# Attention, ELU layer and Sinkhorn mixture on one core: order of the sums' copies, a VectorE transpose for the gate, and four small moves

## The chip, the cores and the metric

The kernel runs on one core of one Trainium2 chip. A core has five engines that each work through their own list of instructions in order: PE (TensorE, matrix products), DVE (VectorE), ACT (ScalarE), POOL (GpSimd) and SP (SyncE, here only a queue that issues DMAs). They wait for one another by semaphores. The metric is the device time of one execution in microseconds (us); less is better.

## The reference

```python
# attention: B=4, H=8, S=576, D=64, causal window of 64
scores = where(0 <= i - j < 64, q @ k.T / 8, -1e9)
x = softmax(scores) @ v                      # -> 2304 tokens x 512
# layer 1: 512 -> 2048 -> 512 with ELU
h = x @ w_in;  x = elu(h) @ w_out
# layer 2: 8 experts, 512 -> 1024 -> 512
P = exp(x @ w_gate - max)
for _ in range(8):                           # Sinkhorn
    P /= P.sum(1, keepdims=True) + 1e-9
    P /= P.sum(0, keepdims=True) + 1e-9
    P *= N / E
out = sum over e of P[:, e] * (relu(x @ w1[e]) @ w2[e])
```

The weights `w_in` and `w_out` come as float64 and are turned into float32 on the chip. Each float32 operand is split into a high and a low part, and each product is done as three products (high x high, high x low, low x high).

## The kernel before

The 2304 tokens are five blocks, four of 512 and the last of 256. Program order per engine is written out by hand, so what stands in an engine's list is what the code emits, in that order.

Attention (to about 180 us) works on 48 groups, two in each step `m`. In a step the code emits transposes of q and k (`pair_T`, tiles `ptr`, `qkT`), scores (`grp_S`, tile `s`), exponentials (`grp_E`), and products with v (`grp_V`, tile `pv`). V is needed a second time shifted by 64 rows: `v_load` brings `vo`, `v_shift` makes `ve` from it, by GpSimd for the first two pairs of heads and by two DMAs on SP's queue after that. For every third pair `vo` is a part of the tile `acc`. `warm(n)` emits products of zeros. Chunks of layer 1 fill the slots between.

Layer 1's first quarter ends with the last block: `m0_in` and `m0_out` (tiles `p`). `elu` makes the activated block `gh` and its low part `gl`, spread over three later moments (`run_later`). Between the last block's first and second products one chunk of the next quarter, `step_in(steps[0])`, is emitted.

The gate follows layer 1 block by block: `gate_a` makes the logits transposed (`lg`, 16 rows of which 8 are of the weights' high and 8 of their low part), `gate_b` turns them by products with a small selection matrix `sel` into `Lg`, tokens by experts. `sink_parts` is then a list of small steps, maximum (`mx`, `nb`), exponential, and alternately `rows` and `cols`, that are emitted one at a time between chunks of layer 2. `cols` sums over tokens by a product (`csum`) and makes the factor `rc`.

The last stage (from about 866 us) does the experts by a Strassen-like scheme. For each of 38 periods there are 14 first-layer chunks `l1` (six products of 384 columns into `la` or `lb`) and 7 second-layer products `l2` (18 products of 256 columns into `oa` or `ob`), two chunks and one product a step `s`, the products `LAG` steps behind. After a chunk ScalarE keeps a copy of its accumulator (`keep`: `a`, `u`, `v`; and `r`), and only then may the next chunk into the same accumulator run. VectorE makes sums from these (`c`, `s`), and of each sum ScalarE makes the high part `h` (`hid`), VectorE or GpSimd the low part (`hid_low`); those are what the second-layer products read. The list `after` holds work that is emitted behind the next chunk; in the kernel before it holds the last sum of each half period alone.

SP's list is in program order too, and a DMA that waits there holds up all behind it.

Of the kernel before, what the change touches and what calls it, by code (L numbers as in the profile page):

```python
# [8 lines left out]
F32 = mybir.dt.float32  # L9
# [9 lines left out]
def kernel(  # L19
# [42 lines left out]


    mask = const.tile([P, P], F32, name="mask")
    sel = const.tile([2 * E, E], F32, name="sel")
    gwr = const.tile([P, NCC, E], F32, name="gwr")
    pad_cm, pad = pool("pad", side="right")
    ctx.callback(close, pad_cm)
# [42 lines left out]
    def ps_sm(name):  # L111
        return ps.tile([P, 512], F32, tag="sm", bufs=1, name=name)
# [144 lines left out]
    def pair_load(pi):  # L257
        b, hp = divmod(pi, NPAIR)
        h0 = 2 * hp
        t = {}  # L260
        for z, (nm, src) in enumerate((("q", q), ("k", k))):
            if pi % 3 == 2:
                w = NTQ * 2 * D
                x = acc[3][:TQ, z * w:(z + 1) * w].rearrange("p (t h d) -> p t h d", h=2, d=D)
            else:
                x = at.tile([TQ, NTQ, 2, D], F32, tag="nat", bufs=4, name=f"{nm}n")
            for h in range(2):
                nc.sync.dma_start(
                    out=x[:, :, h, :],
                    in_=src[b, h0 + h].rearrange("(t p) d -> p t d", p=TQ),  # L270
                )
            t[nm] = x
        qk_nat[pi] = t
# [267 lines left out]
    def moe1_out(st, extra):  # L541
        step_out(st)
        u, j, i = st
        if u == NU - 1 and i == UF - 1:
            fs = [
                lambda: (x2_store(j), x2_split(j, (0, 1))), lambda: x2_split(j, (2, 3)),
                lambda: None, lambda: gate_a(j), lambda: gate_b(j),
            ]
            logits.append(fs[3])
            gate_fs.extend(fs)  # L550
            extra += fs
            if j == len(blocks) - 2:
                extra += sink_parts()


    lgT = {}
# [1 line left out]
    def gate_a(j):  # L558
        n = blocks[j][1]
        lg = ps_sm("lg")  # L560
        for c in range(NCC):
            nc.tensor.matmul(lg[:, :n], gw[:, c, :], Xh[j][:, c, :], start=(c == 0), stop=False)
            nc.tensor.matmul(
                lg[:, :n], gw[:, c, :], Xl[j][:, c, :], start=False, stop=(c == NCC - 1)
            )
        t = work.tile([P, TB], F32, tag="m", bufs=2, name="lgT")[:2 * E]
        nc.vector.tensor_copy(t[:, :n], lg[:2 * E, :n])
        lgT[j] = t

    def gate_b(j):  # L570
        t0, n = blocks[j]
        lt = ps_sm("lt")
        nt = n // P
        t = lgT.pop(j)
        for tt in range(nt):
            nc.tensor.matmul(
                lt[:, tt * E:(tt + 1) * E], t[:, tt * P:(tt + 1) * P], sel, start=True, stop=True
            )
        nc.vector.tensor_copy(
            Lg[:, t0 // P:t0 // P + nt, :], lt[:, :nt * E].rearrange("p (t e) -> p t e", e=E)  # L580
        )

    sk = {}

    def sink_parts():
# [35 lines left out]
        def cols():  # L621
            t = ps_sm("csum")
            nc.tensor.matmul(t[:, :E], ones, sk["cs"], start=True, stop=True)
            rc = sk["rc"]
            nc.vector.tensor_scalar(rc, t[:, :E], 1e-9, None, op0=ALU.add)
            nc.vector.reciprocal(rc, rc)
            nc.vector.tensor_scalar(rc, rc, float(NT) / E, None, op0=ALU.mult)
            nc.vector.tensor_tensor(
                out=Pr, in0=Pr, in1=rc.unsqueeze(1).to_broadcast([P, NTT, E]), op=ALU.mult
            )  # L630
# [402 lines left out]
    def l1(k, n, p, pi):  # L1033
# [27 lines left out]
        def ssum(nm, a, b, op):  # L1061
            d[nm] = tmp("s", 6, nm)
            nc.vector.scalar_tensor_tensor(d[nm], d[a], 0.0, d[b], op0=ALU.max, op1=op)  # L1063

        if pi == 1:
            keep("a")
        elif pi == 2:
            add("c11", "a")
            hid_low(*hid(key, 0, d["c11"], True))
        elif pi == 6:  # L1070
            keep("u")
        elif pi == 5:
            keep("v")
            c = d["C"][:, :TH]
            t = tmp("c", 5, "c22")
            nc.vector.tensor_tensor(out=t, in0=c, in1=d["v"], op=ALU.add)  # L1076
            d["c22"] = t
            hid_low(*hid(key, 2, t, True))
        elif pi == 3:
            d["r21"] = tmp("s", 6, "r21")  # L1080
            nc.scalar.activation(d["r21"], o, AF.Relu)
            ssum("s3", "c11", "r21", ALU.subtract)
            h3 = hid(key, 5, d["s3"], False)
            ssum("s1", "c22", "r21", ALU.add)
            ssum("s2", "c11", "s1", ALU.subtract)
            h2 = hid(key, 4, d["s2"], False)
            h1 = hid(key, 3, d["s1"], False)
            for h in (h3, h2, h1):
                hid_low(*h)
        elif pi == 4:  # L1090
            add("c21", "u")
            h1 = hid(key, 1, d["c21"], True)
            ssum("s4", "c21", "s2", ALU.add)
            hid_low(*h1)
            after.append(lambda: hid_low(*hid(key, 6, d["s4"], False)))
            del chains[key]


# [50 lines left out]
    with tc.manual_schedule():  # L1149
# [25 lines left out]
        warm(8)  # L1175
        for n in range(2):
            pair_T(n)
            warm(2)
        for kk in range(2 * UF):
            bg += w_tasks(kk)  # L1180
        NGRP = B * NPAIR * NG
# [31 lines left out]
        for m in range(NST + 3):  # L1213
# [23 lines left out]
                grp_N(mid)  # L1237
            for n in nxt:
                pair_T(n)
            for n in old:  # L1240
                if n > NG and n % NG == 0:
                    v_shift(n // NG)
            if fin:
                pv = ps_ac("pv")
# [10 lines left out]
                bg += [w_tasks(2 * UF + x)[0] for x in range(2)]  # L1255
            run_bg(rate[1])
            run_later()
            for n in new:
                if n and n % NG == 0:
                    v_load(n // NG)  # L1260
            for pi in range(3, B * NPAIR):
                if 3 * pi // 2 - 4 == m:
# [8 lines left out]
        nc.gpsimd.tensor_tensor(  # L1271
            out=gw[:, :, E:2 * E], in0=gwr, in1=r(gw[:, :, 0:E]), op=ALU.subtract
        )
        nc.vector.tensor_copy(sel[0:E, :], ident[0:E, 0:E])
        nc.sync.dma_start(out=sel[E:2 * E, :], in_=ident[0:E, 0:E])
        run_bg(len(bg))
        bg += [w_tasks(2 * UF + m)[1] for m in range(2)]
        for kk in range(2 * UF + 2, 4 * UF):
# [5 lines left out]
        while avail:  # L1284
            for _ in range(min(2, len(avail))):
                if avail[0][:2] == ("o", len(blocks) - 1) and not queue:
                    step_in(steps[0])
                    queue.append(steps[0])
                    run_later()
                run_sub(avail.pop(0))  # L1290
            run_bg(2)
            run_later()
            run_bg(2)
            run_later()
# [6 lines left out]
        for s, st in enumerate(steps):  # L1301
            u, j, i = st
            su = s % per_u
            if su == 0 and u + 1 < NU:
                for kk in range(2 * UF):
                    bg += w_tasks(2 * UF * (u + 1) + kk)
            if s:
                step_in(st)
                queue.append(st)
            rate = 0 if su < 3 else 5  # L1310
# [108 lines left out]
        for s in range(NPD * 7 + LAG):  # L1419
            k, j = divmod(s, 7)  # L1420
            if k < NPD:
                for z, (p, pi) in enumerate(pairs[j]):
                    l1(k, s * 2 + z, p, pi)
                    if pi != 4:
                        while after:
                            after.pop(0)()
                    w1_load(s * 2 + z + NW1)
            while after and k >= NPD:
                after.pop(0)()
            if s == LAG - 1:  # L1430
                l2(0, 0)
            elif s > LAG:
                l2(*divmod(s - LAG, 7))
# [50 lines left out]
```

## Time and profile before

| | before |
|---|---|
| three runs, us | 2008.22, 2011.4 (median), 2015.02 |
| profiled execution, us | 2014.06 |
| its span, us | 2011.6 |
| PE busy in it | 1989.5 us, 99% |
| DVE, ACT, POOL busy | 69%, 43%, 38% |
| DMA, mean over the span | 239 GB/s |

The span is from the first to the last instruction of the profiled execution; its own time is 2.5 us longer. A share of busy time is a mean over stages that differ: attention fills ACT, the normalisation fills DVE, and most of the rest fills PE.

### The profile page before, as it was taken

What the parts mean: (1) busy time and instruction counts of PE and PEld (TensorE: products, weight loads), DVE (VectorE), ACT (ScalarE), POOL (GpSimd) and SP (SyncE); (2) the same over time, 40 slices, a digit from 0 to 9 for tenths busy, and PEclk for the clock granted to TensorE, in tenths of its full rate; (3) what the DMA queues carried; (4) which work ended last, traced back from release to release, by engine and by line L of the source; (5) the groups of instructions that cost most, each with busy time, mean ns of one, the idle gap of its engine ahead of it and who ended that gap; (6) DMA issues with size and microseconds to landing.
All of it is one profiled execution on the core that took longest, in us unless ns stands there. A gap on an engine that the chain in (4) does not pass through costs nothing.

```text
span 2011.6 us, 36449 instructions
## 1 busy us (share of the span) xinstructions
PE 1989.5 (99%) x13190; PEld 1844.9 (92%) x13190; DVE 1394.1 (69%) x2727; ACT 860.6 (43%) x1839; POOL 755.7 (38%) x725
## 2 busy tenths in 40 slices
PE   9999999999999999999999999999999999999998
PEld 7778888898888888889999999999999999999998
DVE  6745676767698665657776776767777767777676
ACT  8766455555443443333343333333333333333332
POOL 5323232334255555343363332332344323333332
PEclk9999999999999999999999999999999999999999
DMA  9751254458599999958878878778788788887784
GB/s 212 160 106 40 76 177 155 164 187 294 203 364 337 369 364 367 333 196 270 277 247 270 250 250 247 252 250 248 247 276 274 247 245 250 250 250 248 249 247 128
DMA packets 290866, 481.59 MB, mean 239 GB/s; under 512 B 78528, under 2 KB 145152, under 8 KB 286848
## 3 DMA queue, kind: packets, MB, share of 16 engines
q1 hardware_dynamic: 290608, 479.24, 74.7%
q8 instruction: 105, 1.72, 0.3%
q14 instruction: 73, 0.60, 0.1%
q10 hardware_dynamic: 80, 0.03, 0.0%
HBM read 348.14 MB, written 126.88 MB: 236 GB/s over the span
## 4 chain that ended last, share of the span: by engine, by line
PE 83%; DVE 5%; issue 4%; DMA 3%; ACT 3%; POOL 1%; SPq 1%; DVEq 0%; POOLq 0%; ACTq 0%
PE la L1046 15%; PE oa L1119 13%; PE ob L1119 13%; PE lb L1046 11%; PE ac L884 2%; PE ac L883 2%; PE ac L885 2%; PE p L867 2%; PE p L866 2%; PE p L865 2%; PE p L205 2%; PE p L206 2%; PE p L204 2%; PE ac L532 2%; PE ac L533 2%
## 5 line engine op out<-in xcount | busy, mean ns | idle before, releaser
L1028 POOL TENSOR_TENSOR h<-s,h 128x384 fp32r<-128x384 f32 x304 | 373.4, 1246 | 714.4 <-ACT h L1019 506.6
L1046 PE MATMUL la<-xf,w1f 128*128 128x384 f32 x1824 | 363.1, 337 | 6.8 <-ACT u L1059 6.2
L1046 PEld LDWEIGHTS la<-xf,w1f 128*128 128x128 f32 x1824 | 312.6, 189 | 9.8 <-ACT u L1059 8.6
L1119 PE MATMUL oa<-w2f,h 128*128 128x256 f32 x2394 | 307.3, 282 | 0.8 <-DVE acc L1140 0.8
L1119 PE MATMUL ob<-w2f,h 128*128 128x256 f32 x2394 | 307.2, 282 | 0.0
L1119 PEld LDWEIGHTS oa<-w2f,h 128*128 128x128 f32 x2394 | 302.0, 190 | 1.0 <-DVE acc L1140 1.0
L1119 PEld LDWEIGHTS ob<-w2f,h 128*128 128x128 f32 x2394 | 302.0, 190 | 0.0
L1024 DVE SCALAR_TENSOR_TENSOR h<-c,h 128x384 fp32r<-128x384 f32 x228 | 194.2, 852 | 129.9 <-ACT h L1019 120.9
L1046 PE MATMUL lb<-xf,w1f 128*128 128x384 f32 x1368 | 275.1, 335 | 0.2 <-DVE c L1076 0.2
L1046 PEld LDWEIGHTS lb<-xf,w1f 128*128 128x128 f32 x1368 | 237.7, 189 | 0.7 <-DVE c L1076 0.7
L1019 ACT ACTIVATE h<-s 128x384 fp32r<-128x384 f32 x304 | 150.7, 519 | 181.2 <-DVE s L1063 101.4
L1140 DVE SCALAR_TENSOR_TENSOR acc<-oa,Pr,acc 128x256 f32<-128x256 f32 x393 | 165.2, 475 | 43.1 <-PE oa L1119 43.1
L1019 ACT ACTIVATE h<-c 128x384 fp32r<-128x384 f32 x228 | 117.8, 517 | 171.7 <-DVE c L1054 113.4
L1140 DVE SCALAR_TENSOR_TENSOR acc<-ob,Pr,acc 128x256 f32<-128x256 f32 x381 | 160.2, 475 | 38.3 <-PE ob L1119 38.3
L704 POOL TENSOR_TENSOR sw<-rw 128x256 f32<-128x256 f32 x110 | 103.8, 943 | 208.5 <-DVE f L734 158.1
L246 ACT ACTIVATE hh<-p 128x512 fp32r<-128x512 f32 (+1 forms) x80 | 39.3, 491 | 196.7 <-PE p L867 196.7
L1059 ACT ACTIVATE v<-la 128x384 f32<-128x384 f32 x76 | 37.4, 492 | 198.2 <-PE la L1046 198.2
L1063 DVE SCALAR_TENSOR_TENSOR s<-c,s 128x384 f32<-128x384 f32 x152 | 98.1, 646 | 16.1 <-DVE s L1063 0.5
L865 PE MATMUL p<-xh,f 128*128 128x512 f32 (+1 forms) x320 | 108.6, 339 | 0.0
L867 PE MATMUL p<-xh,f 128*128 128x512 f32 (+1 forms) x320 | 107.6, 336 | 0.0
L866 PE MATMUL p<-xl,f 128*128 128x512 f32 (+1 forms) x320 | 107.5, 336 | 0.0
L247 DVE SCALAR_TENSOR_TENSOR hl<-p,hh 128x512 fp32r<-128x512 f32 (+1 forms) x80 | 44.3, 556 | 89.7 <-ACT hh L246 89.7
(159 smaller groups left out, 3639.6 us busy)
## 6 DMA issues: line engine op xcount, KB each, us to landing
w1f<-wdi SPq DMA_DIRECT2D x532, 256.0 KB, 3.8
w2f<-wdo SPq DMA_DIRECT2D x266, 512.0 KB, 4.1
wdo<-f SPq DMA_DIRECT2D x28, 1024.0 KB, 7.4
rw<-in_moe_w_dram SPq DMA_DIRECT2D x220, 128.0 KB, 4.4
wdi<-f SPq DMA_DIRECT2D x27, 1024.0 KB, 6.8
wdo<-f SPq DMA_DIRECT2D x28, 768.0 KB, 5.3
wdi<-f SPq DMA_DIRECT2D x27, 768.0 KB, 5.0
raw<-in_moe_w_in_dram SPq DMA_DIRECT2D x16, 512.0 KB, 4.4
```

Source lines behind the costliest of these rows:

```text
L247: nc.vector.scalar_tensor_tensor(gl[:, :n], p1[:, :n], 0.0, r(gh[:, :n]), op0=ALU.max, op1=ALU.subtract)
L704: nc.gpsimd.tensor_tensor(out=sw[:, o], in0=a, in1=b, op=op)
L865: nc.tensor.matmul(p1[:, :n], w[:, s, 0, cs], xh, start=(c == 0), stop=False)
L866: nc.tensor.matmul(p1[:, :n], w[:, s, 0, cs], xl, start=False, stop=False)
L867: nc.tensor.matmul(p1[:, :n], w[:, s, 1, cs], xh, start=False, stop=(c == NCC - 1))
L1019: nc.scalar.activation(h[:, 0], src, AF.Relu if relu else AF.Copy)
L1024: nc.vector.scalar_tensor_tensor(h[:, 1], src, 0.0, r(h[:, 0]), op0=ALU.max, op1=ALU.subtract)
L1028: nc.gpsimd.tensor_tensor(out=h[:, 1], in0=src, in1=r(h[:, 0]), op=ALU.subtract)
L1046: nc.tensor.matmul(o, w[:, a, c, :], x[:, b, c, :], start=first and c == 0 and z == 0, stop=last and c == 1 and z == 2, skip_group_check=True,
L1063: nc.vector.scalar_tensor_tensor(d[nm], d[a], 0.0, d[b], op0=ALU.max, op1=op)
L1119: nc.tensor.matmul(o[:, c * HB2:(c + 1) * HB2], hs[p][:, a, c * P:(c + 1) * P], w[:, p, b, :], start=fresh and c != 1 and p == 0 and z == ...
L1140: nc.vector.scalar_tensor_tensor(a, src, pe, a, op0=ALU.mult, op1=ALU.add)
```

## The change

Six edits:

1. Start: the first pair's k is loaded from ScalarE's DMA queue; the two `warm(2)` behind the first two transposes are gone.
2. Third V (pair 2): loaded and shifted one step `m` sooner.
3. Last block of layer 1: two chunks, `steps[:2]`, instead of one stand between its two kinds of products; the main loop then starts at the third.
4. Gate: VectorE transposes 32 rows of the logits in blocks of 32x32, adds the two parts into the attention's `mask` tile, and four DMAs on SP's queue put them into `Lg`. `sel` and the `lt` products are gone.
5. Sinkhorn: one more empty step ahead of it; `cols` does its factor in one VectorE instruction fewer.
6. Last stage: all sums' copies go through `after` (`put`), behind the next chunk's own `keep`, but for the chunk `pi == 4`, which lets them wait for one chunk more; the first second-layer product is done at step `LAG - 3` instead of `LAG - 1`.

```diff
-    sel = const.tile([2 * E, E], F32, name="sel")
+    const.tile([P, E], F32, name="gap")
...
-                nc.sync.dma_start(
+                (nc.scalar if pi == 0 and z else nc.sync).dma_start(
...
-                extra += sink_parts()
+                extra += [lambda: None] + sink_parts()
...
-        t = work.tile([P, TB], F32, tag="m", bufs=2, name="lgT")[:2 * E]
-        nc.vector.tensor_copy(t[:, :n], lg[:2 * E, :n])
-        lgT[j] = t
+        t = work.tile([P, TB], F32, tag="m", bufs=2, name="lgT")[:32]
+        nc.vector.transpose(t[:, :n], lg[:32, :n])
+        v = t[:, :n].rearrange("p (t q e) -> p t q e", q=4, e=32)
+        u = mask[:32, :n // 4].rearrange("p (q t e) -> p q t e", q=4, e=E)
+        nc.vector.tensor_tensor(
+            out=u.rearrange("p q t e -> p t q e"), in0=v[:, :, :, 0:E], in1=v[:, :, :, E:2 * E],
+            op=ALU.add,
+        )
+        lgT[j] = u
...
-        for tt in range(nt):
-            nc.tensor.matmul(
-                lt[:, tt * E:(tt + 1) * E], t[:, tt * P:(tt + 1) * P], sel, start=True, stop=True
+        u = lgT.pop(j)
+        for q in range(4):
+            nc.sync.dma_start(
+                out=Lg[32 * q:32 * q + 32, t0 // P:(t0 + n) // P, :], in_=u[:, q]
             )
-        nc.vector.tensor_copy(
-            Lg[:, t0 // P:t0 // P + nt, :], lt[:, :nt * E].rearrange("p (t e) -> p t e", e=E)
-        )
...
-            nc.vector.tensor_scalar(rc, t[:, :E], 1e-9, None, op0=ALU.add)
+            nc.vector.tensor_scalar(
+                rc, t[:, :E], 1e-9, float(E) / NT, op0=ALU.add, op1=ALU.mult
+            )
             nc.vector.reciprocal(rc, rc)
-            nc.vector.tensor_scalar(rc, rc, float(NT) / E, None, op0=ALU.mult)
...
+        def put(slot, nm, relu):
+            after.append(lambda: hid_low(*hid(key, slot, d[nm], relu)))
+
...
-            hid_low(*hid(key, 0, d["c11"], True))
+            put(0, "c11", True)
...
-            hid_low(*hid(key, 2, t, True))
+            put(2, "c22", True)
...
             ssum("s3", "c11", "r21", ALU.subtract)
-            h3 = hid(key, 5, d["s3"], False)
             ssum("s1", "c22", "r21", ALU.add)
             ssum("s2", "c11", "s1", ALU.subtract)
-            h2 = hid(key, 4, d["s2"], False)
-            h1 = hid(key, 3, d["s1"], False)
-            for h in (h3, h2, h1):
-                hid_low(*h)
+            put(5, "s3", False)
+            put(4, "s2", False)
+            put(3, "s1", False)
...
-            warm(2)
...
-            for n in old:
-                if n > NG and n % NG == 0:
+            for n in mid if m == 4 else old:
+                if n > NG and n % NG == 0 and (n // NG > 2 or m == 4):
                     v_shift(n // NG)
...
-            for n in new:
-                if n and n % NG == 0:
+            for n in nxt if m == 2 else new:
+                if n and n % NG == 0 and (n // NG != 2 or m == 2):
                     v_load(n // NG)
...
-                    step_in(steps[0])
-                    queue.append(steps[0])
-                    run_later()
+                    for st in steps[:2]:
+                        step_in(st)
+                        queue.append(st)
+                        run_later()
+                        run_later()
...
-            if s:
+            if s > 1:
                 step_in(st)
...
                 for z, (p, pi) in enumerate(pairs[j]):
+                    fs = list(after) if pi != 4 else []
+                    del after[:len(fs)]
                     l1(k, s * 2 + z, p, pi)
-                    if pi != 4:
-                        while after:
-                            after.pop(0)()
+                    for f in fs:
+                        f()
...
-            if s == LAG - 1:
+            if s == LAG - 3:
                 l2(0, 0)
```

What this does to the engines' lists shows in three places. First, ScalarE at the start of the last stage, from the copy `r` of the first half period to the copy `v` of the second (`h<-c` and `h<-s` are high parts of sums). Before:

```order
L1081 ACTIVATE r_9239<-la 128x384
L1019 ACTIVATE h_9243<-s_9241 128x384
L1019 ACTIVATE h_9249<-s_9247 128x384
L1019 ACTIVATE h_9251<-s_9245 128x384
L1019 ACTIVATE h_9266<-c_9264 128x384
L1019 ACTIVATE h_9284<-c_9282 128x384
L1019 ACTIVATE h_9287<-s_9268 128x384
L1059 ACTIVATE u<-la 128x384
L1059 ACTIVATE v<-la 128x384
```

And of the change:

```order
L1086 ACTIVATE r_9220<-la 128x384
L1021 ACTIVATE h_9253<-s_9222 128x384
L1021 ACTIVATE h_9256<-s_9226 128x384
L1021 ACTIVATE h_9259<-s_9224 128x384
L1021 ACTIVATE h_9262<-c_9236 128x384
L1021 ACTIVATE h_9265<-s_9238 128x384
L1061 ACTIVATE u<-la 128x384
L1021 ACTIVATE h_9278<-c_9251 128x384
L1061 ACTIVATE v<-la 128x384
```

The copy of the second half's first sum, the second `h<-c`, has moved from ahead of `u` to behind it; five copies of the first half's sums still stand ahead of `u`.

Second, PE at the same place, from the chunk behind which `u` is copied to the first second-layer product (its first two rows; `la` and `lb` are chunks). Before:

```order
L1046 MATMUL la<-xf_9071,w1f 128x384 x6
L1046 MATMUL la<-xf_9074,w1f 128x384 x6
L1046 MATMUL lb<-xf_9077,w1f 128x384 x6
L1046 MATMUL la<-xf_8995,w1f 128x384 x6
L1046 MATMUL lb<-xf_9028,w1f 128x384 x6
L1119 MATMUL ob<-w2f,h_9179 128x256 x3
L1119 MATMUL ob<-w2f,h_9284 128x256 x3
```

And of the change:

```order
L1048 MATMUL lb<-xf_9016,w1f 128x384 x6
L1048 MATMUL la<-xf_9052,w1f 128x384 x6
L1121 MATMUL ob<-w2f,h_9170 128x256 x3
L1121 MATMUL ob<-w2f,h_9278 128x256 x3
L1121 MATMUL ob<-w2f,h_9170 128x256 x3
```

The second-layer product has moved ahead of four chunks, of which the first two end the first period and the next two begin the second.

Third, VectorE at the fourth full block's logits, which are the last, and the first step of the Sinkhorn part behind them (`hl`: low part of a layer 2 chunk; `f`: low parts of expert weights). Before:

```order
L567 COPY lgT<-lg 16x512
L247 SCALAR_TENSOR_TENSOR hl<-p_6130,hh 128x512
L579 COPY Lg<-lt 128x32
L591 TENSOR_REDUCE mx<-Lg 128x1
L734 TENSOR_TENSOR f_6167<-rw,f_6167 128x4x256
```

And of the change:

```order
L567 STREAM_TRANSPOSE lgT<-lg 32x512
L570 TENSOR_TENSOR mask<-lgT 32x4x4x8
L247 SCALAR_TENSOR_TENSOR hl<-p_6121,hh 128x512
L736 TENSOR_TENSOR f_6154<-rw,f_6154 128x4x256
L736 TENSOR_TENSOR f_6154<-sw,f_6154 128x4x256
L736 TENSOR_TENSOR f_6171<-rw,f_6171 128x4x256
L736 TENSOR_TENSOR f_6171<-sw,f_6171 128x4x256
L736 TENSOR_TENSOR f_6188<-rw,f_6188 128x4x256
L247 SCALAR_TENSOR_TENSOR hl<-p_6201,hh 128x256
L736 TENSOR_TENSOR f_6188<-sw,f_6188 128x4x256
L247 SCALAR_TENSOR_TENSOR hl<-p_6238,hh 128x256
L901 TENSOR_TENSOR acc_103<-ac,acc_103 128x512 x4
L592 TENSOR_REDUCE mx<-Lg 128x1
```

The reduction `mx`, the first reader of all of `Lg`, has moved behind six `f`, two `hl` more and the four additions into `acc`.

## Rows read from the trace of the kernel before

**Rows 1.** The page, part 1: busy time of each engine over the span.

```profile
PE 1989.5 (99%) x13190; PEld 1844.9 (92%) x13190; DVE 1394.1 (69%) x2727; ACT 860.6 (43%) x1839; POOL 755.7 (38%) x725
```

**Rows 2.** What PE waited for, whole span: us in total, times, longest us.

```profile
PE la L1046 <- ACT u L1059: 6.2, 6, 2.5
PE csum L623 <- DVE cs L619: 2.0, 2, 1.5
PE pv L412 <- DMA ve<-vo: 1.9, 1, 1.9
PE p L485 <- DVE gl L235: 1.6, 2, 0.8
```

**Rows 3.** Timeline of the first 8 us: start us, length us, engine, line, [idle before].

```profile
5.79 0.55 PE L316 MATMUL ptr<-ident,kn 96*128 96x96 f32 x2 [0.23 <-DMA kn<-in_k_dram]
6.04 1.02 PE L1173 MATMUL warm<-gw 128*128 128x512 f32 x2
6.37 0.49 ACT L322 ACTIVATE qkT<-ptr 128x384 f32<-128x384 f32 x1 [2.35 <-PE ptr L316]
...
7.83 0.77 PE L348 MATMUL s<-qkT 64*64 64x64 f32 x12
```

**Rows 4.** Timeline of VectorE, 211 to 220 us.

```profile
218.37 1.60 DVE L235 TENSOR_TENSOR gl<-m,gh 128x512 fp32r<-128x512 f32 x2
```

**Rows 5.** Timeline of PE about the last `lt` products, 549 to 551 us.

```profile
549.55 0.39 PE L884 MATMUL ac<-f,hh 128*128 128x512 f32 x1
549.78 0.39 PE L885 MATMUL ac<-f,hl 128*128 128x512 f32 x1
550.10 1.05 PE L576 MATMUL lt<-sel,lgT 16*128 16x8 f32 x8
551.08 0.39 PE L865 MATMUL p<-xh,f 128*128 128x256 f32 x1
```

**Rows 6.** Tiles `lgT`, `ve`; SP's and VectorE's timeline; a window; line 627.

```profile
L567 DVE COPY lgT<-lg x5: 405/672/680, 453.9 to 546.1; 16x512 f32<-16x512 f32 x4, 16x256 f32<-16x256 f32 x1
...
DMA to landing us min/median/max: 2.4/4.1/6.1
...
541.28 4.74 SPq L690 DMA_DIRECT2D rw<-in_moe_w_dram  x4
...
562.78 2.47 DVE L899 TENSOR_TENSOR acc<-ac,acc 128x512 f32<-128x512 f32 x4
...
567.00:612.00 45.00, 43.05 (x217) 36.07 (x217) 42.52 (x96) 19.17 (x26) 20.92 (x26) 1.00 1.00 372
...
L627 DVE TENSOR_SCALAR rc<-rc x8: 171/346/721, 572.7 to 616.1; 128x8 f32<-128x8 f32 x8
```

**Rows 7.** Window 880.6 to 887.3 us: PE, PEld, DVE, ACT, POOL, granted clock, DMA.

```profile
880.60:887.30 6.70, 5.87 (x17) 5.36 (x18) 1.85 (x4) 1.78 (x5) 0.84 (x1) 0.50 0.78 272
```

**Rows 8.** Timeline at the start of the last stage, ScalarE and PE.

```profile
879.43 0.52 ACT L1019 ACTIVATE h<-c 128x384 fp32r<-128x384 f32 x1 [1.70 <-DVE c L1054]
...
880.27 0.47 ACT L1059 ACTIVATE u<-la 128x384 f32<-128x384 f32 x1
...
880.79 2.29 PE L1046 MATMUL la<-xf,w1f 128*128 128x384 f32 x6 [2.47 <-ACT u L1059]
...
883.72 2.29 PE L1046 MATMUL la<-xf,w1f 128*128 128x384 f32 x6 [0.64 <-ACT v L1059]
```

**Rows 9.** Timeline at 991 to 999 us, ScalarE and PE.

```profile
992.35 1.20 PE L1046 MATMUL la<-xf,w1f 128*128 128x384 f32 x6
...
993.38 2.31 PE L1119 MATMUL ob<-w2f,h 128*128 128x256 f32 x18
...
995.53 1.21 PE L1046 MATMUL lb<-xf,w1f 128*128 128x384 f32 x6
...
997.39 0.47 ACT L1059 ACTIVATE u<-la 128x384 f32<-128x384 f32 x1
...
997.92 1.34 PE L1046 MATMUL la<-xf,w1f 128*128 128x384 f32 x6 [1.17 <-ACT u L1059]
```

More of the change, by code (lines that the diff above doesn't have):

```diff
@@ L565, in gate_a @@
             )
-        t = work.tile([P, TB], F32, tag="m", bufs=2, name="lgT")[:2 * E]
-        nc.vector.tensor_copy(t[:, :n], lg[:2 * E, :n])
-        lgT[j] = t
+        t = work.tile([P, TB], F32, tag="m", bufs=2, name="lgT")[:32]
[7 more added lines that the diff above has]
+        lgT[j] = u
     def gate_b(j):
         t0, n = blocks[j]
-        lt = ps_sm("lt")
-        nt = n // P
-        t = lgT.pop(j)
-        for tt in range(nt):
-            nc.tensor.matmul(
-                lt[:, tt * E:(tt + 1) * E], t[:, tt * P:(tt + 1) * P], sel, start=True, stop=True
-            )
-        nc.vector.tensor_copy(
-            Lg[:, t0 // P:t0 // P + nt, :], lt[:, :nt * E].rearrange("p (t e) -> p t e", e=E)
-        )
+        u = lgT.pop(j)
+        for q in range(4):
+            nc.sync.dma_start(
+                out=Lg[32 * q:32 * q + 32, t0 // P:(t0 + n) // P, :], in_=u[:, q]
+            )
     sk = {}
@@ L1082, in l1 @@
             ssum("s3", "c11", "r21", ALU.subtract)
-            h3 = hid(key, 5, d["s3"], False)
             ssum("s1", "c22", "r21", ALU.add)
             ssum("s2", "c11", "s1", ALU.subtract)
-            h2 = hid(key, 4, d["s2"], False)
-            h1 = hid(key, 3, d["s1"], False)
-            for h in (h3, h2, h1):
-                hid_low(*h)
+            put(5, "s3", False)
+            put(4, "s2", False)
+            put(3, "s1", False)
         elif pi == 4:
             add("c21", "u")
-            h1 = hid(key, 1, d["c21"], True)
             ssum("s4", "c21", "s2", ALU.add)
-            hid_low(*h1)
-            after.append(lambda: hid_low(*hid(key, 6, d["s4"], False)))
+            put(1, "c21", True)
+            put(6, "s4", False)
             del chains[key]
@@ L1273 @@
         )
-        nc.vector.tensor_copy(sel[0:E, :], ident[0:E, 0:E])
-        nc.sync.dma_start(out=sel[E:2 * E, :], in_=ident[0:E, 0:E])
         run_bg(len(bg))
```

## The prediction, made before the changed kernel ran

> **What bounds the kernel now.** I read the page's busy line first. TensorE (PE) is busy 1989.5 of 2011.6 us [rows 1], so 22 us of the span are all that is idle on it, and no other engine is above 69%. A saving can then only come from three places: PE instructions that are taken out, PE idle time, and stretches in which PE is busy but slow. The list of PE's waits says where the idle time is: 6.2 us in six waits for ScalarE's copy `u`, 2.0 us of `csum` for VectorE, 1.9 us of `pv` for a DMA, 1.6 us of `p` for `gl` [rows 2]. Then I went to each of these places in the timeline and read what ended last there. The sum below is made against the profiled execution, 2014.06 us at a span of 2011.6; that is 2.7 us above the median of the three runs, 2011.4.
>
> **Start.** PE's own sequence sets the pace: it makes the first transposes, waits 0.23 us for `kn`, does two warm-up products (from 6.04 us), and starts the first scores at 7.83, although `qkT` was copied at 6.37 + 0.49 = 6.86 [rows 3]. Without the warm-up products between, the scores can start near 6.9, and earlier by the 0.23 us if k's loads no longer stand behind q's on SP's queue. Bounds: 0 (ScalarE later eats it) and 1.2 us. I take 1.0, because the loads behind k on SP's queue come sooner as well. The two DMA issues on ScalarE's queue stand ahead of an ACT that does its first copy only at 6.37. The third V: its two shift DMAs and its three loads move ahead of other issues on SP's queue. The one wait of `pv` for a shift is for `ve<-vo` [rows 2], whereas the third V's shift reads `acc`; it has no wait to remove, and costs nothing as long as the q and k loads that now stand behind it land before their transposes. I count 0.
>
> **Last block's products.** PE waits 1.6 us in two pieces for `gl` [rows 2], the halves of the activated block that VectorE writes, the later one of them in the pair from 218.37 [rows 4]. The change puts a second chunk ahead of them: 12 products of 128x512 at 0.23 us spacing (549.55 to 549.78) [rows 5], that is 2.7 us, taken from behind the products and not added. Both waits are shorter than that. Bounds 0 and 1.6; I take 1.6. What is late next would be the weights of the third chunk, wanted some 1.6 us sooner.
>
> **Logits.** The 36 small `lt` products go. Eight of them hold PE from the product at 549.78 to the one at 551.08, 1.30 us where 0.23 is normal [rows 5]: 1.07 us for eight, 36 / 8 x 1.07 = 4.8 us, in a stage where PE has no cover to hide them in. I take 4.8 (4.0 to 4.8). In their place VectorE transposes and adds. The old copy took 0.67 us for 512 columns [rows 6]; the transpose is on no row, so I bound it by that copy and by twice it, 1.3 us, for each of five, and take the lower end, as the same columns are read from the same memory. The 20 small DMAs go through SP's queue. The last four stand behind loads that are issued until 541.28 + 4.74 = 546.0; shifts between the same kinds of memory landed after 2.4 to 6.1 us [rows 6]. So they are there by some 556, if four issues take 2 us and VectorE's add a further 1 to 2. The first reader, `mx`, now stands behind the four `acc` additions that began at 562.78 [rows 6]: ample. Queued behind these DMAs are `wdo` stores and the next loads; those loads waited for other engines anyway.
>
> The Trainium skill speaks against these copies: its page "DMA: Bandwidth & Descriptors" (Specifications) asks for at least 512 bytes in a piece, and these are 128 bytes or less. By that rule they could land late, which is rival (d) with its time; no row shows copies of this size, and the same page (Why small descriptors are slow) limits the penalty to HBM, which these copies do not touch. By the rows' landings the sum stays.
>
> **Normalisation.** From 567 to 612 us VectorE is busy 42.52 of 45 [rows 6]: here it is the bound, and PE's `csum` waits are its lateness. Eight `rc` multiplications of 346 ns median leave, about 2.8 us [rows 6]. Against 2.0 us of `csum` waits [rows 2] I take a gain of 1.0: everything starts one step later and the waits may reappear in another place. Bounds: 2.0 us worse, as many as there are now again, and 2.0 us better.
>
> **Start of the last stage.** Here PE stands 2.47 us because `u` is queued on ScalarE behind an `h<-c` that itself waited 1.70 us for VectorE, and then 0.64 us for `v` [rows 8]. In that pause the granted clock fell to 0.50, that is 1.2 GHz, for the 6.7 us to 887.3 [rows 7]; before, PE had run without a break. Six products took 2.29 us there [rows 8] and take 1.20 later [rows 9]. Outside the 0.64 us wait half of that stretch is lost: (6.7 - 0.64) / 2 = 3.0. Together 2.47 + 0.64 + 3.0 = 6.1. With the change each `keep` copy goes ahead of the sums' copies of its own chunk, and the first second-layer product comes two steps sooner, right behind the chunk for which `v` is copied. I leave 1.0 us as remaining, two copies of 0.5 us [rows 8], because five copies still stand ahead of `u` and, two chunks later, of the next one with no second-layer product between. Gain 5.1 (2.1 to 6.1): the lower end is the case that the shorter pause still lowers the clock.
>
> **Rest of the last stage.** The same wait stands five more times, 6.2 - 2.47 = 3.7 us; one is the 1.17 us before 997.92, again with `u` behind `h<-c` [rows 2, 9]. Gain 3.7 (2.0 to 3.7).
>
> **Sum.** 1.0 + 1.6 + 4.8 + 1.0 + 5.1 + 3.7 = 17.2 us: 2014.1 - 17.2 = 1996.9. From the median it would be 1994.2. I forecast 1996: between them, since the stretch at the lower clock need not be in every execution.
>
> **Rivals.**
> (a) The forecast, 1990 to 2002: chance 0.68.
> (b) The waits come back elsewhere. For: ScalarE's five copies now come in one burst behind `a`. If the two last terms are only half there, 4.4 us less: 2001. With the end of the normalisation 2 us worse too: 2004. Chance 0.14.
> (c) The clock rises later at the start. For: four products of PE activity are taken away there, and no row shows the start without them. Against: from 1.45 us to the transposes PE stays as busy as it was. If PE's work of the first 20 us runs at half speed for 10 us more, some 5 to 8 us are lost: 2002 to 2005. Chance 0.08. The Trainium skill, "TensorE: Matmul & The Clock Gate" (Part 1: The HAM clock gate), says that the throttled clock is the default and activity releases it; by that alone the warm-up products should stay. The row at 880 agrees that a pause lowers the clock.
> (d) The change does not do what it says in the logits: VectorE, full in the normalisation, is held by the DMAs' landing and gives the 4.8 us back. Then 2001 to 2002; to lose all, the last copies would have to land 10 us later than the longest landing shown. Chance 0.06.
> (e) Slower. The burst of five copies, 5 x 0.5 = 2.5 us [rows 8], stands between `a` and the next `u` in every one of 38 periods. In that time PE does a chunk (992.35 to 993.38, 1.03 us), a second-layer product (to 995.53, 2.15 us) and another chunk [rows 9], 4.2 us in all, so it is hidden in the steady state. Should the burst wait for VectorE beyond 4.2 us, PE pays each period: 1 us each is 38 us, 2035 in all; it ends slower from about 0.6 us a period. Chance 0.04.
>
> **Numbers.** A measurement of this kernel tells 0.3%, 6 us, from no change: faster is under 2005.4. (a) is below it, as are nearly all of (b), most of (c) and (d): 0.85. Within 0.3%: 0.11, from the upper ends of (b) to (d). Slower 0.04, (e). The range 1988 to 2005 holds (a) with its bounds (all terms at their upper ends, 1.2 + 1.6 + 4.8 + 2.0 + 6.1 + 3.7 = 19.4, from the median give 1992, and 3 to 4 us for the spread of the runs) and (b) to (d).
>
> **What would show it.** Right: no `lt` rows, no `u` wait of PE in the last stage over 0.6 us, full clock through 880 to 887, `csum` waits at or under 1 us, first scores near 6.9 us. Wrong: a PE wait for an `h` or for `Lg`, a granted clock of 0.50 after 8 us, or PE waits that return in each period.

## The result and the profile after

The changed kernel takes 1995.61 us (median of six executions, 1993.22 to 1997.71), the kernel before, beside it, 2012.0 us (2008.22 to 2015.02). The ratio is 0.992, with a 95% interval of 0.9907 to 0.9933. It is faster, within 0.4 us of the forecast. The profiled execution took 1997.08 us at a span of 1995.3.

The page's busy line answers to [rows 1]:

```profile
PE 1978.5 (99%) x13150; PEld 1838.6 (92%) x13150; DVE 1370.3 (69%) x2718; ACT 851.7 (43%) x1839; POOL 733.1 (37%) x725
```

The list of PE's waits (us in total, times, longest) answers to [rows 2]:

```profile
PE ac L531 <- DVE acc L493: 3.0, 1, 3.0
PE ac L885 <- DVE acc L901: 2.1, 1, 2.1
PE warm L1175 <- DVE gw L1170: 1.5, 1, 1.5
PE s L348 <- ACT qkT L322: 1.4, 3, 0.9
PE pv L412 <- DMA ve<-vo: 1.1, 2, 0.8
PE oa L1121 <- DVE acc L1142: 0.8, 1, 0.8
PE la L1048 <- ACT u L1061: 0.7, 2, 0.4
```

The `u` waits of the last stage are 0.7 us in two pieces where they were 6.2 in six, and `csum` and `gl` are gone from the list. New are two waits for `acc`, VectorE's additions to an accumulator, 3.0 us in the gate's stage and 2.1 us where the experts begin. The timeline of ScalarE and PE at the start of the last stage, which answers to [rows 8], and three windows (PE, PEld, DVE, ACT, POOL, granted clock, DMA share, GB/s) that answer to [rows 7]:

```profile
871.52 0.51 ACT L1021 ACTIVATE h<-c 128x384 fp32r<-128x384 f32 x1
871.97 0.53 ACT L1021 ACTIVATE h<-s 128x384 fp32r<-128x384 f32 x1
872.40 0.47 ACT L1061 ACTIVATE u<-la 128x384 f32<-128x384 f32 x1
...
872.92 1.31 PE L1048 MATMUL la<-xf,w1f 128*128 128x384 f32 x6 [0.30 <-ACT u L1061]
...
883.01 2.18 PE L1048 MATMUL la<-xf,w1f 128*128 128x384 f32 x11 [0.38 <-ACT u L1061]
```

```profile
503.85:507.27 3.42, 3.12 (x7) 2.48 (x8) 3.42 (x6) 0.48 (x1) 2.47 (x4) 0.50 1.06 368
872.00:880.00 8.00, 7.70 (x50) 7.38 (x49) 6.15 (x11) 3.08 (x9) 3.39 (x3) 1.00 1.03 394
880.00:887.00 7.00, 6.62 (x44) 6.30 (x43) 5.71 (x8) 4.69 (x11) 4.56 (x4) 1.00 0.93 316
```

At 872 us six products take 1.31 us, where they took 2.29 [rows 8]: the clock stays at 2.4 GHz through the start of the last stage. It falls to 1.2 GHz in another place, for 3.42 us from 503.85, in the new pause of PE.

To see where the 16 us came from, take the start of the same PE product in both timelines. The difference is PE's lead over the kernel before:

| product | before | after | lead |
|---|---|---|---|
| first `pv` that waits for `ve` | 40.13 | 40.00 | 0.13 |
| the next such `pv` | 52.26 | 50.84 | 1.42 |
| `p`, behind the last block's products | 225.03 | 221.29 | 3.74 |
| `p`, behind two blocks' logits | 487.45 | 481.91 | 5.54 |
| `ac`, behind the new wait at 504 | 508.21 | 507.27 | 0.94 |
| `p`, behind all blocks' logits | 551.08 | 546.75 | 4.33 |
| `p`, behind the wait at 560 | 570.17 | 566.93 | 3.24 |
| `p`, behind the last `csum` of before, the seventh of the changed kernel | 613.14 | 607.21 | 5.93 |
| `la`, behind the start of the last stage | 893.91 | 883.01 | 10.90 |
| `la`, behind the last wait of the list | 1624.98 | 1608.91 | 16.07 |

The lead grows at every edit, but 4.6 us of it are lost near 504 (3.1 by the wait, 1.5 while the clock is low behind it) and 1.1 near 560. The chain of waits of the changed kernel says what ended last there (start, length, what):

```profile
484.68 5.87 DMA wdo<-f
...
490.70 1.07 ACT f L731
491.80 1.23 DVE f L736
...
502.18 1.23 DVE f L736
503.40 0.61 DVE acc L493
504.02 0.14 issue
504.15 0.76 PE ac L531
```

ScalarE's fold of a weight part (`f`, lines 731 and 736: a rounded copy, and VectorE's remainder beside it) waits until the store of an earlier part has landed. VectorE takes its instructions in order, so its additions `acc`, which free the PSUM bank for PE's `ac`, stand behind that fold. The kernel before has the same wait of VectorE, 5.82 us, but PE came to this `ac` at 506.63, 1.1 us after `acc` had begun. Lines of the three timelines of before, and then of `acc` and `ac` in the changed kernel:

```profile
492.81 1.06 ACT L729 ACTIVATE f<-rw 128x1024 fp32r<-128x1024 f32 x1 [5.74 <-DMA wdo<-f]
...
493.90 1.22 DVE L734 TENSOR_TENSOR f<-rw,f 128x1024 fp32r<-128x1024 f32 x1 [5.82 <-ACT f L729]
...
505.52 2.48 DVE L493 TENSOR_TENSOR acc<-ac,acc 128x512 f32<-128x512 f32 x4
...
506.63 0.39 PE L531 MATMUL ac<-gh,w1h 128*128 128x512 f32 x1
```

```profile
503.32 2.48 DVE L493 TENSOR_TENSOR acc<-ac,acc 128x512 f32<-128x512 f32 x4
...
504.15 0.76 PE L531 MATMUL ac<-gh,w1h 128*128 128x512 f32 x1 [3.04 <-DVE acc L493]
```

That `ac` starts 0.83 us after `acc` has begun (503.32 to 504.15) when it waits for it, so the room was 0.3 us.

Seven weight parts are folded into two slots by turns, 0, 1, 0, 1, 0, 1, 0, and the eighth goes to slot 0 again. It must wait for the store of the seventh. Whether this explains the lost lead is what the experiments ask first.

### The profile page after: what moved, and what is told of

Its sections match the earlier page's. It is cut to its first block, busy times and chain, and to the rows that moved or that the text cites. A ratio compares the mean times of both kernels' runs of the same rounds, so it can differ in the third digit from the quotient of the medians.

```text
span 1995.3 us, 36342 instructions
## 1 busy us (share of the span) xinstructions
PE 1978.5 (99%) x13150; PEld 1838.6 (92%) x13150; DVE 1370.3 (69%) x2718; ACT 851.7 (43%) x1839; POOL 733.1 (37%) x725
## 3 DMA queue, kind: packets, MB, share of 16 engines
q8 instruction: 105, 1.72, 0.4%
## 4 chain that ended last, share of the span: by engine, by line
PE 92%; ACT 3%; DVE 2%; DMA 2%; issue 1%; SPq 0%; DVEq 0%; ACTq 0%
PE la L1048 16%; PE ob L1121 14%; PE oa L1121 14%; PE lb L1048 11%; PE p L867 3%; PE p L868 3%; PE p L869 3%; PE ac L886 3%; PE ac L885 3%; PE ac L887 3%; PE ac L531 2%; PE ac L533 2%; PE ac L532 2%; PE p L204 2%; PE p L206 2%; PE p L205 2%
## 5 line engine op out<-in xcount | busy, mean ns | idle before, releaser
L1030 POOL TENSOR_TENSOR h<-s,h 128x384 fp32r<-128x384 f32 x304 | 348.6, 1176 | 726.2 <-PE lb L1048 377.2
L1026 DVE SCALAR_TENSOR_TENSOR h<-c,h 128x384 fp32r<-128x384 f32 x228 | 176.7, 776 | 93.3 <-ACT h L1021 92.3
L1086 ACT ACTIVATE r<-la 128x384 f32<-128x384 f32 x76 | 37.4, 492 | 177.0 <-PE la L1048 176.9
```

The costliest lines, as they stand in the source:

```text
L1026: nc.vector.scalar_tensor_tensor(h[:, 1], src, 0.0, r(h[:, 0]), op0=ALU.max, op1=ALU.subtract)
L1030: nc.gpsimd.tensor_tensor(out=h[:, 1], in0=src, in1=r(h[:, 0]), op=ALU.subtract)
```

## Experiments

Each ran beside the kernel before, whose medians were 2011.06 (e1 to e4), 2011.53 (e5 to e8) and 2012.32 (e9 to e12). The changed kernel ran beside its own, 2012.0. So where a run is compared with the changed kernel by medians, the ratios to before give up to 0.7 us more or less, and differences of 1 to 1.5 us are not clear of the spread.

**e1: the last stage's edit alone.** The kernel before, with

```diff
+        def put(slot, nm, relu):
+            after.append(lambda: hid_low(*hid(key, slot, d[nm], relu)))
...
-            hid_low(*hid(key, 0, d["c11"], True))
+            put(0, "c11", True)
...
+                    fs = list(after) if pi != 4 else []
+                    del after[:len(fs)]
                     l1(k, s * 2 + z, p, pi)
...
-            if s == LAG - 1:
+            if s == LAG - 3:
```

> The kernel before with the last stage's edit alone (copies of sums behind the product's own copy, first second-layer product two steps sooner). Theory A, the last stage pays for itself and does not depend on the earlier edits: the lead of TensorE over before grew by 5.0 us at the stage's start and 5.2 us behind it, so 2012.0 - 10.2 = 2001.8. Rival, the prediction's own sizes: 5.1 + 3.7 = 8.8, 2003.2. Rival, a part of the 10 us came from loads that the earlier edits had brought forward: 2005 or more, with waits for u left over 1 us.

Measured: 2003.15 us (2002.09 to 2003.95), ratio 0.9955 (0.9942 to 0.9967), 9 us by the ratio and 7.9 by the medians. PE's waits in it:

```profile
PE csum L623 <- DVE cs L619: 2.0, 2, 1.5
PE p L485 <- DVE gl L235: 1.6, 2, 0.8
...
PE la L1046 <- ACT u L1059: 0.7, 2, 0.4
```

The other edits' waits are all still there, and the `u` waits are the 0.7 us of the full change. This stage pays for itself: about half of the gain is here. The median agrees best with the prediction's 8.8.

**e2: the old logits in the changed kernel**, `gate_a` and `gate_b` as before, `sel` back.

```diff
-        nc.vector.transpose(t[:, :n], lg[:32, :n])
+        nc.vector.tensor_copy(t[:, :n], lg[:2 * E, :n])
...
-            nc.sync.dma_start(
-                out=Lg[32 * q:32 * q + 32, t0 // P:(t0 + n) // P, :], in_=u[:, q]
-            )
+            nc.tensor.matmul(
+                lt[:, tt * E:(tt + 1) * E], t[:, tt * P:(tt + 1) * P], sel, start=True, stop=True
+            )
```

> The changed kernel with the old logits (copy and 36 small products). Theory A, the turned logits' 5.2 us of lead are eaten by the new wait near 504 us (3.04 us and a stretch at half clock, 4.6 us of lead in all) and the one at 560: undoing them costs under 1 us, 1995.5 to 1996.8, no wait of ac for acc near 504, and no granted clock of 0.5 there. Rival, the gains add up as the prediction's sum had them: 1995.6 + 4.8 = 2000.4.

Measured: 1997.13 us (1996.34 to 1998.23). The wait near 504 is 0.11 us, the clock does not fall there, and the wait near 560 is 1.2 us. Undoing an edit that saved PE 5.2 us (1.8 and 3.4 in the table) costs 1.5 us, 0.8 by the ratios, so most of it had been lost again.

**e3: the slots by turns from 1.**

```diff
-    order = [(h, i % 2) for i, h in enumerate(others[N1:N1 + N3])]
+    order = [(h, (i + 1) % 2) for i, h in enumerate(others[N1:N1 + N3])]
```

> The changed kernel with the seven stored weight parts put in slots 1,0,1,0,1,0,1 where they were 0,1,0,1,0,1,0, so that the eighth part no longer takes the slot from which the seventh is still being stored. Theory A, the 3.04 us wait near 504 us is VectorE held in order behind that part's fold, which waits for the store to land: the wait and the half clock behind it go, 1995.6 - 4.6 = 1991.0 (1990 to 1993 if the wait near 560 grows in its place). Rival B, VectorE is late there because the Lg copies hold the weights' loads on SP's queue: the wait stays, 1995.6.

Measured: 1992.72 us (1991.82 to 1992.96). The timelines of ScalarE and VectorE, and then the head of the list of PE's waits:

```profile
485.01 1.05 ACT L731 ACTIVATE f<-rw 128x1024 fp32r<-128x1024 f32 x1
...
499.40 2.48 DVE L493 TENSOR_TENSOR acc<-ac,acc 128x512 f32<-128x512 f32 x4
```

```profile
PE ac L885 <- DVE acc L901: 2.1, 1, 2.1
PE s L348 <- ACT qkT L322: 1.8, 3, 1.3
```

The fold that began at 490.70 begins at 485.01 and waits for no DMA; `acc` comes 3.9 us sooner, and the 3.0 us wait and the half clock are gone. Lg's copies stand on SP's queue as before, so rival B falls. The median gains 2.9 us, not 4.6: the executions of the changed kernel differ in this wait (below), and its profiled one is 1.5 us above its median.

**e4: old logits and new slots.** The diffs of e2 and e3 together.

> The changed kernel with the old logits and the slots of e3. Theory A: without turned logits nothing waits near 504, so the slots give nothing: the same as e2 within 0.5 us, some 1996; against e3 the logits are then worth their 4 to 5 us. Rival B: the same as e2 and e3 alike less the logits' 4.8, 2000.

Measured: 1996.48 us (1995.52 to 1997.87), 0.65 under e2. Against e3 the turned logits are now worth 3.8 us, where without the slots they are worth 1.5. That is a little under the 4 to 5 expected. Of the 1.4 us that are missing to 5.2, 0.9 are in the wait near 560: 1.2 us in e4, 2.1 in e3.

**e5: the slots, and the next parts due three clocks later.**

```diff
-            due += [12.0 * (u - 1 + (i + 1) / (5 * n)) for i in range(5 * n)]
+            c0 = 3.0 if u == 1 else 0.0
+            due += [12.0 * (u - 1) + c0 + (12.0 - c0) * (i + 1) / (5 * n) for i in range(5 * n)]
```

> The slots of e3, and the fold tasks of the first four stored-in-place parts of the third unit due three clocks later, which puts VectorE's four acc additions ahead of a fold that waits for GpSimd. Theory: the wait of ac for acc near 555 us (2.11 us in e3) falls under 0.5 us and what is behind it comes as much sooner: 1992.7 - 1.7 = 1991.0. Rival: the same wait returns as one for the row maximum mx or for the bias nb, which stand behind the additions and take Lg: 1992.7, with these waits grown by 1 to 2 us.

Measured: 1992.01 us (1990.98 to 1992.84). The wait near 555 falls from 2.11 to 1.24 us, not under 0.5: `acc` begins at 554.31 where it began at 554.63, because ScalarE's copy `hh` is now what VectorE's `hl`, ahead of `acc`, waits for (2.35 us). PE also came to it 0.55 us later in this profile, after a start at the low clock; in e12, where it comes as early as in e3, `acc` begins at 553.73, 0.9 us sooner than in e3.

**e6: the kernel before with the slots of e3**, the diff of e3.

> The kernel before with the slots of e3 alone. Theory: VectorE's 5.8 us behind the fold's store is covered there (TensorE reaches the same ac product 1.1 us after the acc addition before it has begun, and has no wait), so nothing is gained: the same as before, 2011 within 1.5. Rival: the fold's pace already binds before, 2008 to 2009.

Measured: 2010.04 us (2008.53 to 2012.84), ratio 0.9992 (0.9983 to 1.0002). The fold begins 5.5 us sooner (487.29 where it was 492.81), and nothing comes of it that can be measured. The same edit that is worth 2.9 us behind the change was covered before.

**e7: the old start in the changed kernel.**

```diff
-                (nc.scalar if pi == 0 and z else nc.sync).dma_start(
+                nc.sync.dma_start(
...
             pair_T(n)
+            warm(2)
```

> The changed kernel with the old start (k's loads on SP's queue, two warm-up products behind each of the first two pairs). Theory by the traces: the lead of 0.63 us at the first scores was down to 0.13 at the first product with v, so undoing it costs 0.1 to 0.6: 1995.7 to 1996.2. Rival, the prediction's size: 1.0, 1996.6. Rival, without the warm-up products the clock rises later in some executions (10.9 us in the profile of e2, 4.6 to 5.5 in three others): undone, the clock rises at 6 to 7 us as in the two profiles of the old start, and the median is 0.5 to 1 us better, 1995.

Measured: 1995.29 us (1993.83 to 1996.35), not slower than with the new start. The first two groups of scores, timeline of PE, in the changed kernel, in e8 (the same start) and in e7:

```profile
7.02 0.77 PE L348 MATMUL s<-qkT 64*64 64x64 f32 x12 [0.25 <-ACT qkT L322]
...
8.15 0.87 PE L348 MATMUL s<-qkT 64*64 64x128 f32 x12
```

```profile
6.97 1.33 PE L348 MATMUL s<-qkT 64*64 64x64 f32 x12
...
8.95 1.55 PE L348 MATMUL s<-qkT 64*64 64x128 f32 x12
```

```profile
7.83 0.77 PE L348 MATMUL s<-qkT 64*64 64x64 f32 x12
...
8.97 0.87 PE L348 MATMUL s<-qkT 64*64 64x128 f32 x12
```

Twelve scores take 0.77 us at 2.4 GHz and 1.33 at 1.2 GHz. With the new start, five of nine profiles (after, e3, e4, e9, e10) have them at the high clock and four (e2, e5, e8, e11) at the low one; with the old start all five (before, e1, e6, e7, e12) have them at the high clock. The third group then starts at 9.8 to 10.2 or at 11.5 to 11.8 us, with the old start at 10.9 to 11.0. In the mean of the nine, 10.75 against 10.93, the new start gains 0.2 us there.

**e8: the third V at its old steps.**

```diff
-            for n in mid if m == 4 else old:
-                if n > NG and n % NG == 0 and (n // NG > 2 or m == 4):
+            for n in old:
+                if n > NG and n % NG == 0:
...
-            for n in nxt if m == 2 else new:
-                if n and n % NG == 0 and (n // NG != 2 or m == 2):
+            for n in new:
+                if n and n % NG == 0:
```

> The changed kernel with the third V loaded and shifted at the old steps. Theory by the traces: the wait of pv for ve near 51 us is 0.80 after and 1.89 before, so undoing costs 1.1: 1996.7, with a pv wait of 1.5 to 2.2 us near 52. Rival, the prediction's: no wait hangs on it, 1995.6.

Measured: 1996.93 us (1994.76 to 2000.11), 1.3 over the changed kernel, with executions that overlap its own. The profiled one has a `pv` wait of 0.65 us, not the expected 1.5 to 2.2, but PE came 0.85 us later by the low clock at the start. More can be told from the profiles with the old start, whose first 40 us agree within 0.2 us. The `p` product that starts at 210.07 in the changed kernel starts at 211.05 to 211.55 with the old steps (before, e1, e6) and at 210.19 and 210.27 with the new (e7, e12): the new steps give 1.1 us.

**e9: the old normalisation, and no empty step ahead of it.**

```diff
-                extra += [lambda: None] + sink_parts()
+                extra += sink_parts()
...
+            nc.vector.tensor_scalar(rc, rc, float(NT) / E, None, op0=ALU.mult)
```

> The changed kernel with the old normalisation (third rc operation back, no empty step ahead of it). Theory by the traces: TensorE's lead grew by 2.7 us between 570 and 613 us, so undoing costs that: 1998.3, with csum waits of 1.5 to 2 us again. Rival, the prediction's size: 1.0, 1996.6. Rival: part of that growth is the wait near 560 being given back behind it, 1997.

Measured: 2001.31 us (1999.54 to 2003.36), 5.7 over the changed kernel, more than any of the three expected. VectorE's timeline, and then PE's waits:

```profile
547.76 0.30 DVE L592 TENSOR_REDUCE mx<-Lg 128x1 f32<-128x144 f32 x1 [3.69 <-DMA Lg<-mask]
...
558.93 2.47 DVE L900 TENSOR_TENSOR acc<-ac,acc 128x512 f32<-128x512 f32 x4
```

```profile
PE ac L884 <- DVE acc L900: 4.1, 1, 4.1
PE csum L624 <- DVE cs L620: 1.8, 2, 1.5
```

Without the empty step the maximum `mx` stands ahead of six folds and of `acc`, and holds VectorE 3.69 us until the last Lg copy has landed. PE then waits 4.1 us for `acc` where it waited 2.1, and its clock falls to 1.2 GHz for 3.4 us. In this profile PE comes out of the place near 504 2.85 us ahead of the changed kernel (its wait there is 1.58 us, without the lower clock), and it is 0.58 us late at the `p` of 567.51: 3.4 us are lost to Lg's landing, where e7 keeps its like lead of 2.5 us. The two `csum` waits are back as well: at the `p` of 611.36 PE is 3.16 us late, 2.6 more. So the 5.7 has two parts, Lg's landing and, a little smaller, the normalisation. Since the run undoes both edits at once, the parts are told apart by their place in the trace alone.

**e10: one chunk ahead of the last block's products.**

```diff
-                    for st in steps[:2]:
-                        step_in(st)
-                        queue.append(st)
-                        run_later()
-                        run_later()
+                    step_in(steps[0])
+                    queue.append(steps[0])
+                    run_later()
```

> The changed kernel with one chunk ahead of the last block's products, as before. Theory by the traces: the lead grew by 2.3 us there, and VectorE's fold behind the gate moves with TensorE (the wait near 504 us fell by only 0.3 us in e8, where TensorE came 0.85 us later): 1995.6 + 2.0 = 1997.6, two gl waits of 0.7 to 0.8 us, the wait near 504 still over 2 us. Rival, the prediction's size: 1.6, 1997.2. Rival, the wait near 504 us eats what comes ahead of it: it falls to about 1 us with no half clock, and the time stays at 1995.6.

Measured: 1996.18 us (1995.6 to 1998.16), 0.6 over the changed kernel. PE's waits:

```profile
PE ac L531 <- DVE acc L493: 1.6, 1, 1.6
PE p L485 <- DVE gl L235: 1.6, 2, 0.8
```

The `gl` waits are back and PE is 2.33 us later behind them, but its wait near 504 is 1.6 instead of 3.0 us, without the lower clock. In the timelines the fold's start, `acc` and PE stand so:

| kernel | fold `f<-rw` starts | first `acc` starts | PE ready for `ac` | PE's wait |
|---|---|---|---|---|
| after | 490.70 | 503.32 | 501.11 | 3.04 |
| e7 | 489.66 | 502.28 | 501.31 | 1.79 |
| e9 | 489.27 | 501.89 | 501.14 | 1.58 |
| e11 | 491.21 | 503.82 | 501.79 | 2.87 |
| e10 | 491.52 | 504.14 | 503.41 | 1.56 |
| e2 | 490.90 | 503.60 | 504.32 | 0.11 |

`acc` follows the fold by 12.6 or 12.7 us in every one. The fold itself comes between 489.3 and 491.5 (491.62 in e8, where PE is ready at 502.33) and follows PE only in part: in e10 and e2 PE is 2.3 and 3.2 us later than after, the fold 0.8 and 0.2. What PE gains ahead of this place it waits for here, and between executions of the same code the wait differs by 1.5 us.

**e11: the second-layer product two steps later again**, the new order of copies kept.

```diff
-            if s == LAG - 3:
+            if s == LAG - 1:
```

> The changed kernel with the first second-layer product two steps later again, the new order of copies kept. Theory, the product's place is what covers ScalarE's burst at the stage's start: the wait for u near 873 us grows from 0.30 to some 2.3 us, the granted clock falls to 0.5 behind it as before, cost 2 to 5 us: 1997.6 to 2000.6. Rival, the order of copies alone does it: under 0.5 us, 1996.

Measured: 1995.51 us (1994.3 to 1998.13), the same as the changed kernel. PE's timeline:

```profile
873.83 1.32 PE L1048 MATMUL la<-xf,w1f 128*128 128x384 f32 x6 [0.30 <-ACT u L1061]
875.78 1.31 PE L1048 MATMUL la<-xf,w1f 128*128 128x384 f32 x6 [0.64 <-ACT v L1061]
```

The `u` wait does not grow. My theory falls: with the new order of the copies the product's place gives nothing, and the earlier product only replaces a wait of 0.64 us for `v` by one of 0.38 us for a later `u`.

**e12: e5 with the old start**, the diffs of e3, e5 and e7 together.

> e5 (slots and due times) with the old start of e7. Theory: no wait near 504 us, the one near 555 at 1.2 us, the clock rises at 6.6 to 7.0 us in the profile: 1991.7, 0.3 under e5, with less spread than the 1.9 us of e5. Rival, the new start's 0.6 us are real in the median: 1992.6.

Measured: 1991.11 us (1990.64 to 1991.35), ratio to before 0.9895 (0.9879 to 0.991). It is the fastest version, 4.5 us under the changed kernel, and its four executions lie within 0.7 us where the four of e5 lie within 1.9.

## Why the prediction was right, and where only its sum was

The time, 1995.61, was forecast as 1996.0, by case (a). The last stage's two terms, half of the sum, were right in mechanism. The others were off in ways that cancelled, so that the sum came as near as 0.4 us is luck: what rival (b) calls waits that come back elsewhere is there, 5.7 us of lead near 504 and 560, and larger gains than forecast made up for it. By the prediction's own steps:

- **Start, 1.0:** mis-sized; 0.13 by the table at 40 us, 0.2 in the mean of the profiles at the third group, and nothing left at the `p` product near 210, where the profiles with the third V's new steps come at 210.3 in the mean with the new start and at 210.2 with the old. The scores did start at 7.02, near the 6.9 foretold. Rival (c), "the clock rises later", holds in four of nine profiles; it was priced at 5 to 8 us and costs some 1.5 at the third group, 1.0 at that `p`. The Trainium skill, "TensorE: Matmul & The Clock Gate" (Part 1: The HAM clock gate), says that the number of products at the low clock at a kernel's start changes from run to run; these profiles agree, for the new start.
- **Third V, 0:** the prediction looked only at the shift that is itself moved. By the table PE gains 1.3 us where a later pair's `pv` waits for `ve`, as that wait falls from 1.89 to 0.80. That wait alone is a poor measure, as it is 0.2 us in e6, with the old steps; but by the profiles compared at e8 the new steps give 1.1 us, so the 0 was wrong.
- **Last block's products, 1.6:** 2.3 in the table, of which the `gl` waits are 1.6. The other 0.7 is in how the list counts: a wait begins at the end of the product ahead, but in an unbroken row the next product starts before that end. In PE's timeline of before

```profile
214.29 0.28 PE L484 MATMUL p<-gh,w1h 128*128 128x256 f32 x1
215.38 0.39 PE L485 MATMUL p<-gl,w1h 128*128 128x256 f32 x1 [0.81 <-DVE gl L235]
215.61 0.28 PE L486 MATMUL p<-gh,w1l 128*128 128x256 f32 x1
215.72 0.27 PE L484 MATMUL p<-gh,w1h 128*128 128x256 f32 x1
```

  the first three starts span 1.32 us where two spacings are 0.23, so the wait of 0.81 us costs 1.09. Taken by itself the edit is worth 0.6 (e10), because the wait at 504 takes the rest.
- **Logits, 4.8:** the first half of the step was right, 5.2 us of PE, and the transpose took what the lower bound had assumed (tile `lgT`: count and nanoseconds; the old copy 0.672 us [rows 6]):

```profile
L567 DVE STREAM_TRANSPOSE lgT<-lg x5: 432/697/704, 450.9 to 542.9; 32x512 f32<-32x512 f32 x4, 32x256 f32<-32x256 f32 x1
```

  The step that failed is "in a stage where PE has no cover to hide them in". PE had none, but VectorE was 0.3 us from being the one that is waited for (e1, which comes there with 0.48 us of lead, already has 0.2 us of this wait). The edit is worth 1.5 us (e2), and 3.8 once the slots are changed (e3, e4). I had asked only what the edit's own DMAs could hold up (rival d), not what else already waited on VectorE with PE just behind it.
- **Lg's copies, hidden:** right in the kernel as changed, since `mx` stands behind `acc`. But the prediction put this down to four `acc` additions only; the empty step, to which it gave no term, is what puts `mx` there. Without it rival (d) happens (e9: 3.69 us on VectorE, 4.1 on PE). The landing itself was as short as assumed, as the view of the tile `Lg` in the changed kernel says of its 20 copies, from issue:

```profile
DMA to landing us min/median/max: 1.6/1.8/4.0
```

  The Trainium skill's page "DMA: Bandwidth & Descriptors" asks for 512 bytes in a piece; by the landings these pieces of 128 bytes or less were not late.
- **Normalisation, 1.0:** mis-sized. The lead grew by 2.7 us (2.5 when the changed kernel's last round, one step later, is over too), and e9 loses 2.6 there. All of it comes at three `csum` products of before: by 0.69 and 1.79 us at the listed waits of 0.41 and 1.54, which again cost more than the list says, and by 0.29 at one too short for the list. So the `csum` waits went whole, and the fear that they reappear, which halved the term, was the error. How much is due to the shorter `cols` and how much to the empty step is not shown, since e9 undoes both.
- **Start of the last stage, 5.1:** 5.0. Of its two causes in the prediction only one was needed: e11 shows that with the new order of the copies the product's place gives nothing. The old order with the new place was not run.
- **Rest of the last stage, 3.7:** 5.2 in the table. The waits are as foretold, and the other 1.5 is again what the list leaves out: the lead grows by 1.44 us at the wait of 1.17 [rows 9], and by 5.1 at all five, which are 3.7 in the list. Both terms together were 8.8; e1 measures 9 by the ratio.

One of the signs listed as "wrong" came true, a clock of 0.50 after 8 us, and it is in a place to which the prediction gave no thought. Rival (e), a burst of copies that PE pays for in each period, did not happen: of 38 periods only the start of the stage has a `u` wait.

## What to carry to other kernels

When PE is sped up in a stage, look for the engines that wait there already with nobody behind them: the time between the moment when such an engine lets PE go on and PE's arrival is how much of the gain will be kept. Here a 5.8 us wait of VectorE had 0.3 us of room, so an edit that saved PE 5.2 us gave some 1.5, and a one-line change to another buffer's order, worthless before (e6), became worth 2.9. And on an in-order engine, price where an instruction stands as well as what it costs: `mx` one step earlier cost more than the eight multiplications beside it.

## What the runs showed of the hardware

PE's pause and the clock: pauses of 1.58, 1.79 and 2.11 us left the granted clock at full, those of 2.46 (e6), 2.47 (before), 2.74 (e8), 2.87 (e11), 3.04 (after) and 4.14 us (e9) were each followed by 3.4 us at 1.2 GHz, 6.8 in the kernel before and in e6, where a second pause of 0.64 us fell into it. In the start, the new order of loads with fewer warm-up products did not delay the clock's rise in every execution but made it fall into two groups, at 4.4 to 5.7 us in five profiles and at 10.2 to 10.9 in four, where it was at 6.6 to 7.0 in all five with the old start.

GpSimd's sums of 128x256 take 0.73 us with VectorE idle and 1.60 to 1.72 while VectorE runs its folds (e9, timeline of both from 550 to 557 us). ScalarE's part of a fold waits 4.16 us for such sums at 556.71 in the changed kernel; that their length is what makes the folds near 560 late was not tested.
